# Three edits to a decode step with a streamed key and value cache: 8 KB runs per partition, a column-tiled projection, and the last key group loaded sooner

## The chip, the cores and the metric

One core of a Trainium2 chip. PE is its matrix engine (TensorE; PEld are its weight loads), DVE the vector engine, ACT the scalar engine, SPq the queue of the sync engine that issues the loads; PSUM holds the tiles that PE writes (ktp, S_ps, A_ps and others). The metric is device time in microseconds (us) of one execution. Beside the time, each profiled run has a *span*: from the first to the last instruction of the program. The time is about 1.8 us longer than the span (206.27 against 204.5 in the profiled run of the kernel before). Times are compared with times here, and spans with spans. The profiled run of the kernel before was a long one (206.27 us, where the median is 205.2), so gains of span against it are up to 1.1 us too large; the ratios are of times and do not have this fault.

## The reference, cut to what matters

```
def reference(A_x, A_k_cache, A_v_cache, A_wq, A_wo, B_x, B_w1, B_b1, B_w2, B_b2, gate_w):
    # 8 sequences, 1 query, 16 query heads on 8 key heads of 256, window = last 1024 of 4096 positions
    q = (x @ wq) per head
    k, v = last 1024 positions of the caches, each key head shared by 2 query heads
    a = softmax(q @ k.T / 16) @ v, heads joined, @ wo
    b = gelu(layernorm(x) @ w1 + b1) @ w2 + b2
    g = sigmoid((x * gate_w).sum(-1))
    return g * a + (1 - g) * b          # 8 x 448, bf16
```

wq and wo are the projections into and out of the attention, w1 and w2 the weights of the MLP b. What it costs to read: 64 MiB of keys and values and some 10 MB of weights, 77.7 MB in all, each byte used once.

## The kernel before

Everything is loaded through a ring of 8 KB-per-partition slots (1 MiB each), in one planned order, from one queue. Work on the caches goes in 16 *groups* of four key heads of one sequence; a group has two slots of keys and two of values.

```python
    def kv_loader(src, b, g):                    # one slot: two heads, 4 KB of each in a partition
        def load(t):
            nc.sync.dma_start(
                t[:].rearrange("p (a n) -> p a n", a=2),
                src[b, g : g + 2, kv_base:Sk, :].rearrange("a (p c) d -> p a (c d)", c=NC),
            )
    ...                                          # cut
    for u in range(1, NQ):                       # order of the loads (NQ = 16 groups)
        add_kv("k", A_k_cache, u)
        add_kv("v", A_v_cache, u - 1)
    add_kv("v", A_v_cache, NQ - 1)
    for q in range(NHQ):                         # then wo: three pieces of 896 KB, 448, 224, 224 KB
        ...
    for u in range(1, NQ):                       # the loop
        transpose_keys(u)                        # 64 PE transposes into PSUM, 8 copies out (5 DVE, 3 ACT)
        values(u - 1, *weights(u - 1))           # 64 value matmuls; 8 + 1 selection matmuls before them
        scores(u)                                # 16 matmuls of 512 columns, 4 column tiles of the PE
        softmax(u)                               # DVE maximum, ACT Exp of 1024 columns
    values(NQ - 1, *weights(NQ - 1))
    ...                                          # oT -> pp -> oP: heads regrouped for the projection by wo
    A_ps = ps_misc.tile([NB, D], F32, tag="misc", name="A_ps")
    for q in range(NHQ):
        for j0, j1 in WO_PARTS[q]:
            w = slot("wo", q, j0)
            for j in range(j0, j1):
                nc.tensor.matmul(A_ps[:, :], lhsT=oP[:, j, q, :],          # 8 rows, 448 columns
                                 rhs=w[:, (j - j0) * D : (j - j0 + 1) * D], ...)
    ...                                          # res = g * A_ps + mixb, stored by one DMA
```

## Time and profile before

The median of three runs was 204.73 us (204.66 to 205.67). Span of the profiled run: 204.5 us.

| what, kernel before | value | where it is read |
|---|---|---|
| DMA engines busy | 9 tenths from about 5 to 189 us, 408 GB/s | page, slices; windows |
| a 4096 B packet / an 8192 B packet (wq) | 164 / 311 ns, median | packet records of the trace |
| a group (4 MiB) | 10.2 us | spacing of key transposes |
| last piece of wo landed | 196.7 us | completion marks of the loads |
| projection A_ps | 192.66 to 201.39 us | timeline |

The span in 40 slices of 5.1 us, from the page of the kernel before: busy tenths of PE, granted PE clock, busy share of the DMA engines, and the rate.

```profile
PE   1898697879797979769797979797978797974793
PEclk9996589696969696966969696969696969695569
DMA  5999999999999999999999999999999999999710
GB/s 202 400 424 413 421 407 412 405 405 409 405 412 405 409 409 406 412 405 408 409 406 408 408 410 406 408 409 406 405 409 405 410 405 410 407 414 413 311 40 1
```

The DMA row is at 9 nearly to the end while PE breathes between 6 and 9, and the clock alternates between full and half: from 41 to 184 us the clock records have 1.0 for 6.8 us and 0.5 for 3.4 us by turns, with one longer half of 6.8 us at 88.6 us. In the windows view of the same kernel the last columns are the granted clock, the busy share of the 16 DMA engines (at 1.03 the durations of the packets sum to more than the time of 16 engines, so some overlap) and the rate.

```profile
core 0: us, PE busy (x) PEld busy (x) DVE busy (x) ACT busy (x) POOL busy (x), PEclk, DMA share, GB/s
50.00:75.00 25.00, 21.94 (x369) 17.82 (x368) 14.11 (x29) 11.08 (x14) 0.00 (x0) 0.84 1.03 408
100.00:150.00 50.00, 43.41 (x745) 38.11 (x743) 27.26 (x60) 21.20 (x25) 0.00 (x0) 0.83 1.03 408
```

So the load stream never pauses.

Last, the timeline of the tail (start, duration, engine, line):

```profile
192.18 0.42 DVE L468 CAST oP<-pp 128x256 bf16<-128x256 f32 x1 [0.59 <-PE pp L460]
192.66 8.72 PE L475 MATMUL A_ps<-slot,oP 128*8 128x448 bf16 x32 [0.57 <-DVE oP L468]
201.42 0.67 DVE L482 SCALAR_TENSOR_TENSOR res<-A_ps,g_sb,mixb 8x448 bf16<-8x448 f32 x1 [8.81 <-PE A_ps L475]
202.12 0.31 SPq L490 DMA_DIRECT2D out_dram<-res  x1
```

oP is ready at 192.6, the projection takes 8.7 us, and result and store follow. There are two candidates for what sets the time: the load stream, and the serial tail of compute after it.

### The profile page before, as it was taken

What the parts mean: (1) busy time and instruction counts of PE and PEld (TensorE: products, weight loads), DVE (VectorE), ACT (ScalarE), POOL (GpSimd) and SP (SyncE); (2) the same over time, 40 slices, a digit from 0 to 9 for tenths busy, and PEclk for the clock granted to TensorE, in tenths of its full rate; (3) what the DMA queues carried; (4) which work ended last, traced back from release to release, by engine and by line L of the source; (5) the groups of instructions that cost most, each with busy time, mean ns of one, the idle gap of its engine ahead of it and who ended that gap; (6) DMA issues with size and microseconds to landing.
All of it is one profiled execution on the core that took longest, in us unless ns stands there. A gap on an engine that the chain in (4) does not pass through costs nothing.

```text
span 204.5 us, 6049 instructions
## 1 busy us (share of the span) xinstructions
PE 166.6 (81%) x2734; PEld 133.1 (65%) x2734; DVE 94.3 (46%) x223; ACT 69.8 (34%) x85; POOL 0.8 (0%) x7
## 2 busy tenths in 40 slices
PE   1898697879797979769797979797978797974793
PEld 1798456566666666649595959595958667672531
DVE  6623046273737373706464646464645363633101
ACT  4330025070707070705261616161615343432000
POOL 1000000000000000000000000000000000000000
PEclk9996589696969696966969696969696969695569
DMA  5999999999999999999999999999999999999710
GB/s 202 400 424 413 421 407 412 405 405 409 405 412 405 409 409 406 412 405 408 409 406 408 408 410 406 408 409 406 405 409 405 410 405 410 407 414 413 311 40 1
DMA packets 19801, 78.07 MB, mean 382 GB/s; under 512 B 1440, under 2 KB 1856, under 8 KB 19392
## 3 DMA queue, kind: packets, MB, share of 16 engines
q1 hardware_dynamic: 19600, 77.68, 94.9%
q8 instruction: 21, 0.34, 0.7%
q10 hardware_dynamic: 176, 0.02, 0.1%
q14 instruction: 4, 0.03, 0.0%
HBM read 77.69 MB, written 0.01 MB: 380 GB/s over the span
## 4 chain that ended last, share of the span: by engine, by line
DMA 64%; PE 19%; DVE 8%; ACT 4%; issue 2%; SPq 2%; ACTq 0%
DMA slot<-in_A_k_cache_dram 29%; DMA slot<-in_A_v_cache_dram 28%; DMA slot<-in_A_wq_dram 7%; PE po L357 6%; PE S_ps L305 5%; PE A_ps L475 4%; DVE nmx L317 4%; DVE kt L270 3%; ACT E L320 2%; PE ktp L264 2%; ACT kt L268 2%; PE sm L340 1%; SPq L115 1%; SPq L96 1%; DVE selr L330 1%
## 5 line engine op out<-in xcount | busy, mean ns | idle before, releaser
L264 PEld LDWEIGHTS <-slot 128*128 128x128 bf16 x1024 | 76.0, 115 | 23.6 <-DMA slot<-in_A_k_cache_dram 16.0
L264 PE MATMUL ktp<-ident,slot 128*128 128x128 bf16 x1024 | 82.3, 250 | 9.6 <-DMA slot<-in_A_k_cache_dram 5.0
L270 DVE COPY kt<-ktp 128x1024 bf16<-128x1024 bf16 x80 | 53.1, 687 | 22.1 <-PE ktp L264 21.1
L268 ACT COPY kt<-ktp 128x1024 bf16<-128x1024 bf16 x48 | 47.8, 1012 | 25.0 <-PE ktp L264 24.9
L320 ACT ACTIVATE E<-S_ps,nmx 128x1024 bf16<-128x1024 f32 x16 | 17.8, 1113 | 84.3 <-DVE nmx L317 84.3
L357 PEld LDWEIGHTS <-slot 128*128 128x128 bf16 x1024 | 30.3, 99 | 9.7 <-issue 6.2
L357 PE MATMUL po<-ET,slot 128*128 128x2 bf16 x1024 | 29.3, 163 | 8.0 <-DVE ET L342 5.0
L317 DVE TENSOR_REDUCE nmx<-S_ps 128x1 f32<-128x1024 f32 x16 | 19.6, 1225 | 19.3 <-PE S_ps L305 19.3
L305 PE MATMUL S_ps<-kt,qw 128*2 128x512 bf16 x256 | 24.3, 516 | 0.4 <-DVE qw L291 0.4
L366 DVE TENSOR_TENSOR oT<-po,rb 128x8 bf16<-128x8 f32 x32 | 4.3, 189 | 32.5 <-PE po L357 32.5
L340 PE MATMUL sm<-selr,ones_f 128*128 128x8 f32 x32 | 6.4, 272 | 6.7 <-DVE selr L330 6.6
L340 PEld LDWEIGHTS sm<-selr,ones_f 128*128 128x128 f32 x32 | 5.0, 195 | 8.2 <-DVE selr L330 7.7
L305 PEld LDWEIGHTS <-qw 128*2 128x2 bf16 x256 | 5.4, 93 | 7.2 <-issue 4.5
L475 PE MATMUL A_ps<-slot,oP 128*8 128x448 bf16 x32 | 8.7, 449 | 0.6 <-DVE oP L468 0.6
L333 PE MATMUL sm<-sel,E 128*128 128x8 bf16 x128 | 5.5, 167 | 2.6 <-ACT E L320 2.6
L342 DVE CAST ET<-sm 128x64 bf16<-128x64 f32 x16 | 3.6, 224 | 8.0 <-PE sm L340 8.0
L333 PEld LDWEIGHTS <-E 128*128 128x128 bf16 x128 | 4.9, 97 | 3.5 <-ACT E L320 3.5
L475 PEld LDWEIGHTS <-oP 128*8 128x8 bf16 x32 | 3.3, 105 | 5.7 <-issue 3.4
L281 PE MATMUL qt<-xT,slot 128*128 128x8 bf16 x128 | 4.0, 168 | 2.3 <-DMA slot<-in_A_wq_dram 1.9
L281 PEld LDWEIGHTS <-slot 128*128 128x128 bf16 x128 | 3.8, 104 | 2.5 <-DMA slot<-in_A_wq_dram 2.2
L482 DVE SCALAR_TENSOR_TENSOR res<-A_ps,g_sb,mixb 8x448 bf16<-8x448 f32 x1 | 0.7, 670 | 8.8 <-PE A_ps L475 8.8
L330 DVE TENSOR_SCALAR selr<-sel,rsum 128x8 f32<-128x8 bf16 x16 | 3.7, 232 | 0.6
(58 smaller groups left out, 39.1 us busy)
## 6 DMA issues: line engine op xcount, KB each, us to landing
slot<-in_A_k_cache_dram SPq DMA_DIRECT2D x32, 1024.0 KB, 18.4
slot<-in_A_v_cache_dram SPq DMA_DIRECT2D x32, 1024.0 KB, 18.4
slot<-in_A_wq_dram SPq DMA_DIRECT2D x3, 1024.0 KB
slot<-in_A_wo_dram SPq DMA_DIRECT2D x3, 896.0 KB, 17.9
slot<-in_B_w_dram SPq DMA_DIRECT2D x1, 1008.0 KB, 16.3
slot<-in_B_w_dram SPq DMA_DIRECT2D x1, 896.0 KB, 9.0
slot<-in_B_w_dram SPq DMA_DIRECT2D x1, 560.0 KB, 15.5
slot<-in_A_wq_dram SPq DMA_DIRECT2D x1, 512.0 KB, 16.5
```

What stands on the lines that cost most here:

```text
L264: nc.tensor.transpose(ktp[:, c * P : (c + 1) * P], kn[:, o : o + P], ident[:])
L268: nc.scalar.copy(kt[:, j, :], ktp[:])
L270: nc.vector.tensor_copy(kt[:, j, :], ktp[:])
L281: nc.tensor.matmul(qt[:, k, :], lhsT=w[:, c : c + P], rhs=xT[:, r + half, :], start=(r == 0 and k == 0), stop=(r == NR), skip_group_check= ...
L305: nc.tensor.matmul(S_ps[32 * a : 32 * a + rep, hf * NMM : (hf + 1) * NMM], lhsT=qw[:, j, b, h0 : h0 + rep], rhs=KT[a][:, j, hf * NMM : (hf ...
L317: nc.vector.reduce_max(nmx[:], S_ps[:], axis=AXIS.X, negate=True)
L320: nc.scalar.activation(E[:], S_ps[:], ACT.Exp, bias=nmx[:], scale=1.0, accum_out=rowsum[:])
L330: nc.vector.tensor_scalar_mul(selr[:], sel[:], rsum[:])
L333: nc.tensor.matmul(sm[:, c, :], lhsT=E[:, c * P : (c + 1) * P], rhs=sel[:], start=True, stop=True,)
L340: nc.tensor.matmul(sm[:, NC, :], lhsT=ones_f[:], rhs=selr[:], start=True, stop=True)
L357: nc.tensor.matmul(PO[:, j, rep * a : rep * (a + 1)], lhsT=vn[:, o + j : o + Dh : NJ], rhs=ET[:, c, rep * a : rep * (a + 1)], start=(c == ...
L475: nc.tensor.matmul(A_ps[:, :], lhsT=oP[:, j, q, :], rhs=w[:, (j - j0) * D : (j - j0 + 1) * D], start=(q == 0 and j == 0), stop=(q == NHQ - ...
```

## The change: intent and diff

Three edits, marked R, T and O here. **R**: the two heads of a slot are interleaved over the partitions (even partitions one head, odd partitions the other), so that a partition reads one run of 8 KB instead of two of 4 KB. For that, Exp writes each column twice, a mask (`own`) drops the wrong head, and selection matmuls go from 8 to 16. **T**: the projections (and the MLP's second matmul) are cut into four column tiles of 112 columns, which run side by side; gate and bias follow them onto four partition blocks, and the store becomes four. **O**: the keys of group 15 are loaded and used one group sooner, before the last values.

```diff
R    def load(t):
         nc.sync.dma_start(
-            t[:].rearrange("p (a n) -> p a n", a=2),
-            src[b, g : g + 2, kv_base:Sk, :].rearrange("a (p c) d -> p a (c d)", c=NC),
+            t[:],
+            src[b, g : g + GP, kv_base:Sk, :].rearrange("a (s c) d -> s a (c d)", c=NCK),
         )
R   scores:
-                        rhs=KT[a][:, j, hf * NMM : (hf + 1) * NMM],
+                        rhs=KT[a // GP][:, j, hf * CMM : (hf + 1) * CMM, :, a % GP],
R   softmax:
-            E[:], S_ps[:], ACT.Exp, bias=nmx[:], scale=1.0, accum_out=rowsum[:]
+            E[:].rearrange("p (k a) -> p k a", a=GP),
+            S_ps[:].rearrange("p (k o) -> p k o", o=1).to_broadcast([P, W, GP]),
+            ACT.Exp, bias=nmx[:], scale=1.0, accum_out=rowsum[:],
R   weights:
-        for c in range(NC):
+        for c in range(NCK):                       # 16 selection matmuls instead of 8
-        nc.vector.tensor_copy(ET[:], sm[:, 0:NC, :])
+        nc.vector.tensor_tensor(ET[:], sm[:, 0:NCK, :], own..., op=ALU.mult)
O   loads:
-    for u in range(1, NQ):
-        add_kv("k", A_k_cache, u)
-        add_kv("v", A_v_cache, u - 1)
-    add_kv("v", A_v_cache, NQ - 1)
+    for u in range(1, NQ - 1):
+        add_kv("k", A_k_cache, u)
+        if u < NQ - 2:
+            add_kv("v", A_v_cache, u - 1)
+    add_kv("k", A_k_cache, NQ - 1)
+    for u in range(NQ - 3, NQ):
+        add_kv("v", A_v_cache, u)
O   the loop runs to NQ - 3, then (u = NQ - 2):
+    transpose_keys(u); W0 = weights(u - 1); scores(u); softmax(u)
+    transpose_keys(u + 1); W1 = weights(u); values(u - 1, *W0)
+    scores(u + 1); softmax(u + 1); values(u, *W1); values(u + 1, *weights(u + 1))
T   projection:
-                nc.tensor.matmul(A_ps[:, :], lhsT=oP[:, j, q, :],
-                                 rhs=w[:, (j - j0) * D : (j - j0 + 1) * D], ...)
+                for dst, cols in quads(A_ps):      # 4 x 112 columns, PSUM partitions 0, 32, 64, 96
+                    nc.tensor.matmul(dst, lhsT=oP[:, j, q, :],
+                                     rhs=w[:, o + cols.start : o + cols.stop], ...)
 ... (gate, bias, mlp_out, stores on the four blocks; ring of 18 slots instead of 19: cut)
```

More of the change, by code (lines that the diff above doesn't have):

```diff
@@ L56 @@
     NQ = NB * Hkv // QUAD
-    CD = NC * Dh
+    GP = 2
+    NCK = NC * GP
+    SK = P // GP
     SLOT = 4096
@@ L62 @@
     WO_PARTS = [[(0, NJ8)]] * (NHQ - 1) + [[(0, 4), (4, 6), (6, 8)]]
-    RING = 19
+    RING = 18
+    NMM = 512
+    CMM = NMM // SK
     qscale = float(Dh) ** -0.5
@@ L71 @@
     ring = ctx.enter_context(tc.tile_pool(name="ring", bufs=RING))
-    ktpool = ctx.enter_context(tc.tile_pool(name="ktpool", bufs=8))
-    epool = ctx.enter_context(tc.tile_pool(name="epool", bufs=2))
+    ktpool = ctx.enter_context(tc.tile_pool(name="ktpool", bufs=4))
+    epool = ctx.enter_context(tc.tile_pool(name="epool", bufs=3))
     ps_s = ctx.enter_context(tc.tile_pool(name="ps_s", bufs=1, space=PSUM))
@@ L96, in load @@
             nc.sync.dma_start(
-                t[:].rearrange("p (a n) -> p a n", a=2),
-                src[b, g : g + 2, kv_base:Sk, :].rearrange(
-                    "a (p c) d -> p a (c d)", c=NC
+                t[:],
+                src[b, g : g + GP, kv_base:Sk, :].rearrange(
+                    "a (s c) d -> s a (c d)", c=NCK
                 ),
@@ L161 @@
     gw_b = consts.tile([NB, D], BF16)
-    b2_b = consts.tile([NB, D], BF16)
+    b2_r = consts.tile([1, D], BF16)
     b1_sb = consts.tile([P, NF], BF16)
@@ L166 @@
     )
-    nc.scalar.dma_start(
-        b2_b[:], B_b2.rearrange("(o d) -> o d", o=1).to_broadcast([NB, D])
-    )
+    nc.scalar.dma_start(b2_r[:], B_b2.rearrange("(o d) -> o d", o=1))
     nc.scalar.dma_start(b1_sb[:], B_b1.rearrange("(p c) -> p c", c=NF))
@@ L180, with quads @@
     NX = NR + 2
+    DQ = D // QUAD
+    def quads(ps):
+        return [
+            (ps[32 * i : 32 * i + NB, :], slice(i * DQ, (i + 1) * DQ))
+            for i in range(QUAD)
+        ]
     xz = consts.tile([NB, 2, P], BF16)
@@ L189 @@
     oT = consts.tile([P, Hq, NJ, NB], BF16)
-    g_sb = consts.tile([NB, 1], F32)
-    omg = consts.tile([NB, 1], F32)
-    b2o = consts.tile([NB, D], F32)
-    mixb = consts.tile([NB, D], F32)
-    res = consts.tile([NB, D], BF16)
+    gg = consts.tile([NB, 2], F32)
+    spread = consts.tile([NB, QUAD, 32], F32)
+    gg_s = consts.tile([P, 2], F32)
+    ones_r = consts.tile([1, NB], BF16)
+    mixb = consts.tile([P, DQ], F32)
+    res = consts.tile([P, DQ], BF16)
+    nc.vector.memset(spread[:], 0.0)
+    nc.vector.memset(ones_r[:], 1.0)
     def transposed(dst, src, srcz):
@@ L209 @@
         ident[:].rearrange("p (a s) -> p a s", a=QUAD)[:, :, 0:rep],
+    )
+    par = consts.tile([P, GP], F32)
+    own = consts.tile([P, RQ], F32)
+    nc.vector.reduce_sum(
+        par[:], ident[:].rearrange("p (s a) -> p a s", a=GP), axis=AXIS.X
+    )
+    nc.vector.tensor_copy(
+        own[:].rearrange("p (t a i) -> p t a i", a=GP, i=rep),
+        par[:]
+        .rearrange("p (t a i) -> p t a i", t=1, i=1)
+        .to_broadcast([P, QUAD // GP, GP, rep]),
     )
@@ L246, in norm_and_gate @@
         nc.scalar.activation(gth[:], gl[:], ACT.Tanh, scale=0.5)
-        nc.vector.tensor_scalar(g_sb[:], gth[:], 0.5, 0.5, op0=ALU.mult, op1=ALU.add)
-        nc.vector.tensor_scalar(omg[:], g_sb[:], -1.0, 1.0, op0=ALU.mult, op1=ALU.add)
-        nc.vector.tensor_scalar_mul(b2o[:], b2_b[:], omg[:])
+        nc.vector.tensor_scalar(
+            gg[:, 0:1], gth[:], 0.5, 0.5, op0=ALU.mult, op1=ALU.add
+        )
+        nc.vector.tensor_scalar(
+            gg[:, 1:2], gth[:], -0.5, 0.5, op0=ALU.mult, op1=ALU.add
+        )
+        nc.vector.tensor_copy(
+            spread[:, :, 0:NB],
+            ident[0:NB, 0:NB]
+            .rearrange("p (o b) -> p o b", o=1)
+            .to_broadcast([NB, QUAD, NB]),
+        )
+        gp = ps_misc.tile([P, 2], F32, tag="misc", name="gp")
+        nc.tensor.matmul(
+            gp[:],
+            lhsT=spread[:].rearrange("p i b -> p (i b)"),
+            rhs=gg[:],
+            start=True,
+            stop=True,
+        )
+        nc.vector.tensor_copy(gg_s[:], gp[:])
     KT = {}
@@ L256, in transpose_keys @@
             kn = slot("k", u, s)
-            for a in range(2):
-                kt = ktpool.tile([P, NJ, W], BF16, tag="kt", name="kt")
-                KT[2 * s + a] = kt
+            kt = ktpool.tile([P, NJ, NCK, SK, GP], BF16, tag="kt", name="kt")
+            KT[s] = kt
+            ktf = kt[:].rearrange("p j c s a -> p j (c s a)")
+            for c0 in range(0, NCK, NC):
                 for j in range(NJ):
@@ L262, in transpose_keys @@
                     for c in range(NC):
-                        o = a * CD + c * Dh + j * P
+                        o = (c0 + c) * Dh + j * P
                         nc.tensor.transpose(
@@ L266, in transpose_keys @@
                         )
+                    dst = ktf[:, j, c0 * P : (c0 + NC) * P]
                     if evac[0] % 8 in (2, 4, 7):
-                        nc.scalar.copy(kt[:, j, :], ktp[:])
+                        nc.scalar.copy(dst, ktp[:])
                     else:
-                        nc.vector.tensor_copy(kt[:, j, :], ktp[:])
+                        nc.vector.tensor_copy(dst, ktp[:])
                     evac[0] += 1
@@ L295, in query @@
             )
-    NMM = 512
     def scores(u):
@@ L317, in softmax @@
         nc.vector.reduce_max(nmx[:], S_ps[:], axis=AXIS.X, negate=True)
-        E = epool.tile([P, W], BF16, tag="E", name="E")
+        E = epool.tile([P, W * GP], BF16, tag="E", name="E")
         rowsum = epool.tile([P, 1], F32, tag="rowsum", name="rowsum")
         nc.scalar.activation(
-            E[:], S_ps[:], ACT.Exp, bias=nmx[:], scale=1.0, accum_out=rowsum[:]
+            E[:].rearrange("p (k a) -> p k a", a=GP),
+            S_ps[:].rearrange("p (k o) -> p k o", o=1).to_broadcast([P, W, GP]),
+            ACT.Exp,
+            bias=nmx[:],
+            scale=1.0,
+            accum_out=rowsum[:],
         )
@@ L329, in weights @@
         selr = epool.tile([P, RQ], F32, tag="selr", name="selr")
-        nc.vector.tensor_scalar_mul(selr[:], sel[:], rsum[:])
-        sm = ps_sm.tile([P, NC + 1, RQ], F32, tag="sm", name="sm")
-        for c in range(NC):
+        nc.vector.tensor_scalar(
+            selr[:], sel[:], rsum[:], float(GP), op0=ALU.mult, op1=ALU.mult
+        )
+        sm = ps_sm.tile([P, NCK + 1, RQ], F32, tag="sm", name="sm")
+        for c in range(NCK):
             nc.tensor.matmul(
@@ L339, in weights @@
             )
-        nc.tensor.matmul(sm[:, NC, :], lhsT=ones_f[:], rhs=selr[:], start=True, stop=True)
-        ET = epool.tile([P, NC, RQ], BF16, tag="ET", name="ET")
-        nc.vector.tensor_copy(ET[:], sm[:, 0:NC, :])
+        nc.tensor.matmul(sm[:, NCK, :], lhsT=ones_f[:], rhs=selr[:], start=True, stop=True)
+        ET = epool.tile([P, NCK, RQ], BF16, tag="ET", name="ET")
+        nc.vector.tensor_tensor(
+            ET[:],
+            sm[:, 0:NCK, :],
+            own[:].rearrange("p (o r) -> p o r", o=1).to_broadcast([P, NCK, RQ]),
+            op=ALU.mult,
+        )
         rb = epool.tile([P, RQ], F32, tag="rb", name="rb")
-        nc.vector.tensor_copy(rb[:], sm[:, NC, :])
+        nc.vector.tensor_copy(rb[:], sm[:, NCK, :])
         return ET, rb
@@ L351, in values @@
             vn = slot("v", u, s)
-            for a2 in range(2):
-                a = 2 * s + a2
-                for j in range(NJ):
-                    for c in range(NC):
-                        o = a2 * CD + c * Dh
-                        nc.tensor.matmul(
-                            PO[:, j, rep * a : rep * (a + 1)],
-                            lhsT=vn[:, o + j : o + Dh : NJ],
-                            rhs=ET[:, c, rep * a : rep * (a + 1)],
-                            start=(c == 0),
-                            stop=(c == NC - 1),
-                        )
+            cols = slice(GP * rep * s, GP * rep * (s + 1))
+            for j in range(NJ):
+                for c in range(NCK):
+                    o = c * Dh + j
+                    nc.tensor.matmul(
+                        PO[:, j, cols],
+                        lhsT=vn[:, o : (c + 1) * Dh : NJ],
+                        rhs=ET[:, c, cols],
+                        start=(c == 0),
+                        stop=(c == NCK - 1),
+                    )
             done()
@@ L421, in mlp_out @@
     def mlp_out(hs):
-        bb = ps_misc.tile([NB, D], F32, tag="misc", name="bb")
+        bb = ps_misc.tile([P, DQ], F32, tag="misc", name="bb")
+        nc.vector.memset(bb[:], 0.0)
         for c in range(NF):
             w, o = (slot("w2", 0), c) if c < W2A else (slot("w2", 1), c - W2A)
-            nc.tensor.matmul(
-                bb[:, :],
-                lhsT=hs[:, c, :],
-                rhs=w[:, o * D : (o + 1) * D],
-                start=(c == 0),
-                stop=(c == NF - 1),
+            for dst, cols in quads(bb):
+                nc.tensor.matmul(
+                    dst,
+                    lhsT=hs[:, c, :],
+                    rhs=w[:, o * D + cols.start : o * D + cols.stop],
+                    start=(c == 0),
+                    stop=False,
+                )
+        for dst, cols in quads(bb):
+            nc.tensor.matmul(
+                dst, lhsT=ones_r[:], rhs=b2_r[:, cols], start=False, stop=True
             )
         done(2)
-        nc.vector.scalar_tensor_tensor(
-            mixb[:],
-            in0=bb[:],
-            scalar=omg[:],
-            in1=b2o[:],
-            op0=ALU.mult,
-            op1=ALU.add,
-        )
+        nc.vector.tensor_scalar_mul(mixb[:], bb[:], gg_s[:, 1:2])
     norm_and_gate()
@@ L448 @@
     mlp_out(hs)
-    for u in range(1, NQ):
+    for u in range(1, NQ - 2):
         transpose_keys(u)
@@ L453 @@
         softmax(u)
-    values(NQ - 1, *weights(NQ - 1))
+    u = NQ - 2
+    transpose_keys(u)
+    W0 = weights(u - 1)
+    scores(u)
+    softmax(u)
+    transpose_keys(u + 1)
+    W1 = weights(u)
+    values(u - 1, *W0)
+    scores(u + 1)
+    softmax(u + 1)
+    values(u, *W1)
+    A_ps = ps_misc.tile([P, DQ], F32, tag="misc", name="A_ps")
+    nc.vector.memset(A_ps[:], 0.0)
+    values(u + 1, *weights(u + 1))
     pp = ps_sm.tile([P, HPQ, NJ, NHQ, NB], F32, tag="sm", name="pp")
@@ L468 @@
     nc.vector.tensor_copy(oP[:], pp[:].rearrange("p m j q b -> p (m j) q b"))
-    A_ps = ps_misc.tile([NB, D], F32, tag="misc", name="A_ps")
     for q in range(NHQ):
@@ L474 @@
             for j in range(j0, j1):
-                nc.tensor.matmul(
-                    A_ps[:, :],
-                    lhsT=oP[:, j, q, :],
-                    rhs=w[:, (j - j0) * D : (j - j0 + 1) * D],
-                    start=(q == 0 and j == 0),
-                    stop=(q == NHQ - 1 and j == NJ8 - 1),
-                )
+                for dst, cols in quads(A_ps):
+                    o = (j - j0) * D
+                    nc.tensor.matmul(
+                        dst,
+                        lhsT=oP[:, j, q, :],
+                        rhs=w[:, o + cols.start : o + cols.stop],
+                        start=(q == 0 and j == 0),
+                        stop=(q == NHQ - 1 and j == NJ8 - 1),
+                    )
     nc.vector.scalar_tensor_tensor(
@@ L484 @@
         in0=A_ps[:],
-        scalar=g_sb[:],
+        scalar=gg_s[:, 0:1],
         in1=mixb[:],
@@ L489 @@
     )
-    nc.sync.dma_start(out_f, res[:])
+    for i, (src, cols) in enumerate(quads(res)):
+        eng = nc.sync if i % 2 == 0 else nc.scalar
+        eng.dma_start(out_f[:, cols], src)
 _INS = ['A_x', 'A_k_cache', 'A_v_cache', 'A_wq', 'A_wo', 'B_x', 'B_w1', 'B_b1', 'B_w2', 'B_b2', 'gate_w']
```

## The prediction

> **What bounds it now.** The busy tenths by slices show the 16 DMA engines at 9 from 5 to 188 us at 405-412 GB/s, for 78 MB. The windows view gives 408 GB/s in the steady part, 421 at 20-25 us, where wq arrives in 8 KB rows. In the packet records a 4096 B packet takes 164 ns (median), an 8192 B one 311 ns. One group (4 MiB of keys and values) takes 10.2 us of DMA.
>
> The compute loop is almost as long. In the timeline, groups start their key transposes 10.18-10.23 us apart at 40-84 us with no wait for a DMA: the chain of waits runs scores (1.8 us, at half clock) - maximum 1.24 - Exp 1.1+0.19 - ScalarE copy 0.9 - transposes 0.6 - two VectorE copies 1.3 - selection matmuls, ET - values 1.85. At 102-153 us, with the half clock falling on the transposes, the same loop waits 0.57 us for keys, so it needs about 9.65 us. From the first key transposes of group 14 (165.05 us) to the end are 39.4 us: the last two groups, then a serial tail: A_ps 8.73 us (32 matmuls of 448 columns, mostly at half clock), result 0.67, store 2.4.
>
> **What the change does.**
> 1. 8 KB runs: 64 MiB of keys and values at about 2.46-2.49 us a MiB instead of 2.55: 4-6 us less DMA, a group 9.85-9.95 us.
> 2. Price of it in compute: Exp writes each element twice. [...] Eight more selection pairs, about 42 ns each: +0.34 on PE; ET as a masked product +0.06. Value matmuls: still 64, with 4 columns. [...]
> The Exp lies on the loop: with the scores cold I estimate 11.1 us, with them warm 10.3, with the transposes cold (Exp half hidden) 10.0. Mean about 10.3, against 10.44 before (29.29 to 165.05 us, 13 groups). So the loop becomes compute-bound, DMA waits for ring slots, and most of the DMA gain is lost.
> 3. Projection in four column tiles: four matmuls of 112 columns side by side. Scores already run that way. 128 pairs at about 29 ns (the value pairs' rate) are 3.7 us: -5 us, all on the tail. Result on 128x112: -0.35. Four stores on two queues: +0.3.
> 4. Last keys sooner: group 15's transposes overlap group 14's softmax, values of 14 overlap softmax 15: by adding durations, -1 to -1.5 us.
>
> **Sum.** Group 14 starts at 29.3 + 13 x 10.3 = 163.2; the new tail takes 33.3 us: 196.5 us. If DMA alone bounded it, about 192. I say 196.0, range 191.5 to 201.5. Faster 0.83, same 0.14, slower 0.03.
>
> **What would show it.** 8 KB packets at 311 ns; DMA share under 0.97 in the steady part with PE not waiting for keys; [...] A_ps 3.5-4.5 us; group starts 10.2-10.5 us apart.
>
> **What would make it wrong.** The loop hides Exp better (then DMA-bound, 191-193); the half-clock stretches settle on the scores (11.1 us a group, 205); key packets alternating between two heads slower than wq's; strided kt reads slowing scores; column tiles serialising.

The sum came to 196.5 us, said as 196.0; the stride-two reads of kt the sum took as free. The loop's 11.1, 10.3 and 10.0 us a group, and so the 196.5 and the 205, contain the term for Exp. The trace after gives 0.855 us for it (1968 against 1113 ns) and 0.04 to 0.06 us for the reads. With this 0.855, the 0.06 of ET and the 10.2 us of the loop before, 11.1 is met again, and less the 0.84 us by which the scores of the kernel before are shorter at full clock (1.87 and 1.03 us), 10.3.

## More of the kernel before

In the groups of the page, the columns after the bar are busy time and mean ns of one, then the idle time of the engine before them and what ended most of it.

```profile
L264 PEld LDWEIGHTS <-slot 128*128 128x128 bf16 x1024 | 76.0, 115 | 23.6 <-DMA slot<-in_A_k_cache_dram 16.0
...
L320 ACT ACTIVATE E<-S_ps,nmx 128x1024 bf16<-128x1024 f32 x16 | 17.8, 1113 | 84.3 <-DVE nmx L317 84.3
...
L475 PE MATMUL A_ps<-slot,oP 128*8 128x448 bf16 x32 | 8.7, 449 | 0.6 <-DVE oP L468 0.6
```

PE's weight loads for the transposes wait mostly for keys (16.0 of the 23.6 us in which they sit idle). The projection at the end waits for oP, not for wo.

The runs of the kernel before lie between 204.3 and 206.4 us.

## The result, and the profile after

The changed kernel takes 198.79 us (median of 4, 198.76 to 199.07), the kernel before 205.2 us (median of 4). Ratio 0.969, interval 0.966 to 0.973: faster. A ratio here is the mean time of one kernel's fast runs over the mean of the other's fast runs of the same rounds, so it is not quite the ratio of the medians. The predicted time was 196.0, range 191.5 to 201.5.

The same slices (now of 4.9 us) for the kernel after:

```profile
PE   1699869868686878979596868686868686887662
PEclk9996556999999996799999999999999999997555
DMA  4999999999999999999999999999999999999960
GB/s 170 416 427 406 420 412 414 421 414 424 411 414 419 419 419 416 414 419 419 423 411 411 423 416 423 409 418 423 416 416 413 418 419 419 421 411 416 413 246 23
```

and the windows:

```profile
core 0: us, PE busy (x) PEld busy (x) DVE busy (x) ACT busy (x) POOL busy (x), PEclk, DMA share, GB/s
50.00:75.00 25.00, 18.38 (x367) 15.49 (x364) 13.34 (x28) 13.62 (x14) 0.00 (x0) 0.98 1.01 417
100.00:150.00 50.00, 37.62 (x782) 31.29 (x779) 26.68 (x60) 24.44 (x25) 0.00 (x0) 1.00 1.01 417
```

The clock is at full speed from 85 to 180 us (half from 16 to 33 us and after 180), PE is less busy, and the DMA engines are as saturated as before (share 1.01), at 417 instead of 408 GB/s. The clock is not what gained: the four runs of the kernel after had mean clocks of 0.81, 0.85, 0.87 and 0.90 and times within 0.31 us of each other.

The groups that answer to those above:

```profile
L311 PEld LDWEIGHTS <-slot 128*128 128x128 bf16 x1024 | 66.1, 105 | 33.3 <-issue 28.3
...
L366 ACT ACTIVATE E<-S_ps,nmx 128x2048 bf16<-128x2048 f32 x16 | 31.5, 1968 | 72.2 <-DVE nmx L363 72.2
...
L545 PE MATMUL A_ps<-slot,oP 128*8 128x112 bf16 x128 | 4.3, 290 | 2.8 <-DMA slot<-in_A_wo_dram 2.1
```

Exp takes 1968 ns where it took 1113. Of the 33.3 us in which the weight loads of the transposes sit idle, 28.3 are "issue", waiting that the profile cannot name, so at most 5.0 are a wait for keys (16.0 before); and A_ps now waits for wo. The tail in the timeline:

```profile
186.90 0.42 DVE L537 CAST oP<-pp 128x256 bf16<-128x256 f32 x1 [0.59 <-PE pp L529]
187.38 1.15 PE L545 MATMUL A_ps<-slot,oP 128*8 128x112 bf16 x32 [0.57 <-DVE oP L537]
188.97 0.92 PE L545 MATMUL A_ps<-slot,oP 128*8 128x112 bf16 x32 [0.44 <-DMA slot<-in_A_wo_dram]
191.17 0.92 PE L545 MATMUL A_ps<-slot,oP 128*8 128x112 bf16 x32 [1.28 <-DMA slot<-in_A_wo_dram]
192.31 1.01 PE L545 MATMUL A_ps<-slot,oP 128*8 128x112 bf16 x24 [0.22 <-DMA slot<-in_A_wo_dram]
193.48 0.36 PE L545 MATMUL A_ps<-slot,oP 128*8 128x112 bf16 x8 [0.16 <-DMA slot<-in_A_wo_dram]
193.89 0.34 DVE L552 SCALAR_TENSOR_TENSOR res<-A_ps,gg_s,mixb 128x112 bf16<-128x112 f32 x1 [6.57 <-PE A_ps L545]
194.25 0.68 SPq L562 DMA_DIRECT2D out_dram<-res  x2
```

oP is ready 5.3 us sooner, and A_ps then sits waiting for each piece of wo: it runs when the pieces land, and ends 0.4 us after the last of them (193.44). The end of the chain of waits says the same (start, duration, what):

```profile
159.60 19.96 DMA slot<-in_A_v_cache_dram
179.62 13.82 DMA slot<-in_A_wo_dram
193.48 0.39 PE A_ps L545 x6
193.89 0.34 DVE res L552
```

Finally, what the DMA engines moved. Packets, and those that the page lists as `instruction`, before:

```profile
DMA packets 19801, 78.07 MB, mean 382 GB/s; under 512 B 1440, under 2 KB 1856, under 8 KB 19392
...
q8 instruction: 21, 0.34, 0.7%
```

and after:

```profile
DMA packets 11645, 78.10 MB, mean 396 GB/s; under 512 B 1489, under 2 KB 1890, under 8 KB 3042
...
q8 instruction: 23, 0.38, 0.8%
```

Packets fell from 19801 to 11645. In the packet records, an 8192 B packet took 313 ns (median) in the kernel after, against 164 ns for one of 4096 B before: 4.6% less per byte by these durations, but packets overlap (the share fell from 1.03 to 1.01), and the rate rose by 2.2%. The `instruction` lines matter later.

A table that the views do not print, worked out from the completion marks of each load (each has sixteen; a load is taken as landed at the last of them, and the transposes of the kernel before start 0.05 to 0.23 us after it in the table) and from the starts of the key transposes. "Lag" is the time from the landing of a group's first keys to the first transpose of them:

| group | 3 | 5 | 6 | 7 | 9 | 12 | 13 | 14 | 15 |
|---|---|---|---|---|---|---|---|---|---|
| before: keys landed, us | 49.64 | 70.06 | 80.26 | 92.03 | 112.42 | 143.05 | 153.23 | 165.00 | 175.23 |
| before: lag | 0.20 | 0.20 | 0.21 | 0.23 | 0.05 | 0.05 | 0.05 | 0.05 | 0.05 |
| after: keys landed, us | 49.22 | 69.16 | 79.20 | 90.65 | 110.69 | 140.60 | 152.05 | 162.04 | 167.02 |
| after: lag | 0.23 | 0.62 | 1.58 | 0.31 | 0.61 | 1.22 | 0.05 | 0.11 | 3.17 |

Before, compute starts on every group within 0.25 us of the landing: it follows the stream. After, the stream delivers a group every 9.98 us and the loop takes 10.17, so the lag grows by 0.2 us a group (by 1.0 in group 5, which met a stretch of half clock at 74 us), and is reset twice, where the landings themselves jump by 1.5 us (79.20 to 90.65 is 11.45 us for one group; before it is 80.26 to 92.03 and 153.23 to 165.00). The 3.17 us at group 15 are edit O, which has these keys landed half a group sooner. Two questions follow. Why does a loop that is slower than the stream not cost time? And what are the jumps?

### The profile page after: what moved, and what is told of

Its sections match the earlier page's. It is cut to its first block, busy times and chain, and to the rows that moved or that the text cites. A ratio compares the mean times of both kernels' runs of the same rounds, so it can differ in the third digit from the quotient of the medians.

```text
span 197.0 us, 6578 instructions
## 1 busy us (share of the span) xinstructions
PE 147.7 (75%) x3006; PEld 125.1 (64%) x3006; DVE 94.3 (48%) x230; ACT 82.0 (42%) x85; POOL 0.9 (0%) x7
## 4 chain that ended last, share of the span: by engine, by line
DMA 49%; PE 26%; DVE 16%; ACT 5%; issue 2%; SPq 0%; ACTq 0%
DMA slot<-in_A_v_cache_dram 31%; PE ktp L311 10%; DMA slot<-in_A_wq_dram 8%; DVE kt L318 7%; PE po L414 7%; DMA slot<-in_A_wo_dram 7%; DVE nmx L363 6%; PE S_ps L351 5%; ACT kt L316 4%; DMA slot<-in_A_k_cache_dram 3%; PE sm L393 2%; ACT E L366 1%; DVE ET L395 1%; DVE selr L381 1%; PE bb L484 1%
## 5 line engine op out<-in xcount | busy, mean ns | idle before, releaser
L311 PE MATMUL ktp<-ident,slot 128*128 128x128 bf16 x1024 | 73.9, 232 | 21.6 <-ACT kt L316 15.2
L311 PEld LDWEIGHTS <-slot 128*128 128x128 bf16 x1024 | 66.1, 105 | 33.3 <-issue 28.3
L366 ACT ACTIVATE E<-S_ps,nmx 128x2048 bf16<-128x2048 f32 x16 | 31.5, 1968 | 72.2 <-DVE nmx L363 72.2
L414 PEld LDWEIGHTS <-slot 128*128 128x128 bf16 x1024 | 29.5, 99 | 6.8 <-issue 6.8
L414 PE MATMUL po<-ET,slot 128*128 128x4 bf16 x1024 | 28.1, 164 | 5.3 <-DVE ET L395 5.3
L351 PE MATMUL S_ps<-kt,qw 128*2 128x512 bf16 x256 | 18.1, 402 | 0.4 <-DVE qw L339 0.4
L386 PE MATMUL sm<-sel,E 128*128 128x8 bf16 x256 | 8.8, 167 | 1.7 <-ACT E L366 1.7
L386 PEld LDWEIGHTS <-E 128*128 128x128 bf16 x256 | 8.2, 97 | 1.8 <-ACT E L366 1.8
L395 DVE TENSOR_TENSOR ET<-sm,own 128x128 bf16<-128x128 f32 x16 | 4.7, 291 | 8.2 <-PE sm L393 8.2
L351 PEld LDWEIGHTS <-qw 128*2 128x2 bf16 x256 | 4.7, 82 | 5.2 <-DVE qw L339 0.5
L545 PE MATMUL A_ps<-slot,oP 128*8 128x112 bf16 x128 | 4.3, 290 | 2.8 <-DMA slot<-in_A_wo_dram 2.1
L329 PEld LDWEIGHTS <-slot 128*128 128x128 bf16 x128 | 3.7, 104 | 1.0 <-DMA slot<-in_A_wq_dram 0.6
```

What stands on the lines that cost most here:

```text
L311: nc.tensor.transpose(ktp[:, c * P : (c + 1) * P], kn[:, o : o + P], ident[:])
L329: nc.tensor.matmul(qt[:, k, :], lhsT=w[:, c : c + P], rhs=xT[:, r + half, :], start=(r == 0 and k == 0), stop=(r == NR), skip_group_check= ...
L351: nc.tensor.matmul(S_ps[32 * a : 32 * a + rep, hf * NMM : (hf + 1) * NMM], lhsT=qw[:, j, b, h0 : h0 + rep], rhs=KT[a // GP][:, j, hf * CMM ...
L366: nc.scalar.activation(E[:].rearrange("p (k a) -> p k a", a=GP), S_ps[:].rearrange("p (k o) -> p k o", o=1).to_broadcast([P, W, GP]), ACT.Exp,
L386: nc.tensor.matmul(sm[:, c, :], lhsT=E[:, c * P : (c + 1) * P], rhs=sel[:], start=True, stop=True,)
L395: nc.vector.tensor_tensor(ET[:], sm[:, 0:NCK, :], own[:].rearrange("p (o r) -> p o r", o=1).to_broadcast([P, NCK, RQ]), op=ALU.mult,)
```

## The experiments

Two theories were set against each other. **D**: the load stream sets the time up to the landing of the last piece of wo; after it comes a tail. **C**, my prediction's: the compute loop and its serial tail set it, and the doubled Exp takes most of the DMA gain back. Later came **F**: the jumps in the landings come with the 16384 B packets that the page lists as `instruction` on q8 (21 before, 23 after; the recorded texts call them pages), of which the first, the 9th and the 17th stand out; so the jumps are gone without PE instructions, and come later and fewer with less of them. The kernels with one or two of the three edits were built from the two kernels by taking over all hunks of the marked edits and leaving the others. Ratios are to the kernel before in the same call, with their 95% interval; with a line drawn at 2%, e1 to e4 and e6 count as "same" and e10 as "unclear", so those differences are read from the intervals and the traces.

### One edit or two of the three

**e1_tiles_only**: the kernel before with edit T.

```diff
-                nc.tensor.matmul(A_ps[:, :], ...)               # 448 columns
+                for dst, cols in quads(A_ps): nc.tensor.matmul(dst, ...)   # 4 x 112
```

> The kernel before with the column-tiled projection alone (4 KB runs, old order). Theory D (the DMA stream sets the time up to the landing of the last piece of wo, then a short tail): last piece of wo lands where it did before, 196.7 us, A_ps waits for it, about 3.6 us of tail: span 200 to 200.8, ratio to before 0.980. Rival C (the compute loop and its serial tail set the time): oP still ready at 192.6, A_ps 4.3 us without a wait for wo, span 200.4. The times agree; the theories differ in the wait: D sees A_ps end its idle time on wo landings, C does not.

Measured: span 200.3, time 202.28 us, ratio 0.985 [0.980, 0.990]. A_ps starts at 193.05, the last piece of wo lands at 196.90, A_ps ends at 197.21:

```profile
193.05 2.56 PE L503 MATMUL A_ps<-slot,oP 128*8 128x112 bf16 x96 [0.57 <-DVE oP L495]
195.81 0.95 PE L503 MATMUL A_ps<-slot,oP 128*8 128x112 bf16 x24 [0.20 <-DMA slot<-in_A_wo_dram]
196.94 0.27 PE L503 MATMUL A_ps<-slot,oP 128*8 128x112 bf16 x8 [0.18 <-DMA slot<-in_A_wo_dram]
```

The last two bursts wait for wo. That is D.

**e2_runs_only**: the kernel before with edit R.

```diff
-                src[...].rearrange("a (p c) d -> p a (c d)", c=NC)
+                src[...].rearrange("a (s c) d -> s a (c d)", c=NCK)
```

> The kernel before with 8 KB runs alone (old order, old projection). Both theories: last piece of wo lands at about 193.4 us, 3.3 earlier, but the old serial tail hides most of it: group starts 10.17 us apart put group 15 at about 172.3, its scores end at 182.5, oP at 190.5, A_ps of 8.7 to 10 us follows: span 202 to 203.5, ratio 0.990 to 0.995. If the DMA gain counted in full here: span 201.2 or less.

Measured: span 203.3, time 204.97 us (202.31 to 205.29), ratio 0.995 [0.987, 1.003]: the same within the noise. The last landing came at 192.50, 4.2 us sooner than before (0.9 sooner than expected; a group took 9.93 us), and the old projection hides it:

```profile
191.16 9.01 PE L502 MATMUL A_ps<-slot,oP 128*8 128x448 bf16 x32 [0.57 <-DVE oP L495]
```

**e3_order_only**: the kernel before with edit O.

```diff
-    for u in range(1, NQ):       transpose, values(u - 1), scores, softmax
+    for u in range(1, NQ - 2):   the same; the last two groups interleaved
```

> The kernel before with the last key group sooner alone (4 KB runs, old projection). Last value slot lands at about 188, oP at about 190.3 instead of 192.6; A_ps of 32 matmuls at 0.27 to 0.37 us, most at half clock, 8.7 to 11.9 us: span 202 to 205, ratio 0.988 to 1.002. Theory D: small, as the projection still runs after the last landing. Rival C: my prediction's 1 to 1.5 us, span 203.

Measured: span 201.3, a little under the range expected, time 203.52 us, ratio 0.992 [0.986, 0.998]. A_ps starts at 190.40 instead of 192.66, which is 2.3 us; it also runs 0.9 us shorter, and that is the clock and not the order (see the table below). The last landing stays at 196.75.

**e6_no_runs**: the kernel after without edit R (so T and O).

```diff
-                t[:], src[...].rearrange("a (s c) d -> s a (c d)", c=NCK)
+                t[:].rearrange("p (a n) -> p a n", a=2), src[...].rearrange("a (p c) d -> p a (c d)", c=NC)
```

> The kernel after with the 4 KB runs of before (column tiles and new order kept, Exp not doubled). Theory D: last landing back at 196.7 us, tail 3.6 as after: span 200.3, 3.3 us over after, ratio to before 0.980. Rival C (my prediction: the doubled Exp takes back most of the DMA gain): a shorter Exp pays for the longer DMA, span within 1 us of after's 197.0.

Measured: span 200.8, time 202.37 us, ratio 0.985 [0.981, 0.990]. From its page:

```profile
L349 ACT ACTIVATE E<-S_ps,nmx 128x1024 bf16<-128x1024 f32 x16 | 17.8, 1114 | 79.5 <-DVE nmx L346 79.5
...
L517 PE MATMUL A_ps<-slot,oP 128*8 128x112 bf16 x128 | 4.0, 291 | 3.4 <-DMA slot<-in_A_wo_dram 3.2
```

Exp is back at 1.11 us, and nothing is gained by it: A_ps waits for wo, the last landing is at 197.31 and A_ps ends at 197.71. Against the kernel after the span is 3.8 us longer; C had expected the two within 1 us. C falls here.

**e4_no_tiles**: the kernel after without edit T (so R and O).

```diff
-                for dst, cols in quads(A_ps): nc.tensor.matmul(dst, ...)
+                nc.tensor.matmul(A_ps[:, :], ...)
```

> The kernel after with the old projection of 32 matmuls of 448 columns (8 KB runs and new order kept). oP ready at 187.4 us as after, then 8.7 us (clock as before) to 11.9 us (all at half clock), result 0.67, store 2.4: span 199.2 to 202.4, 2 to 5.4 us over after's 197.0. If the tiles were worth nothing because wo lands late (last at 193.4): span 197 to 198.

Measured: span 200.2, time 202.92 us (201.92 to 204.31), ratio 0.987 [0.980, 0.995]. The last landing is at 192.60, A_ps runs from 189.66 to 197.05.

**e5_no_order**: the kernel after without edit O (so R and T).

```diff
-    the last two groups interleaved
+    for u in range(1, NQ): transpose, values(u - 1), scores, softmax
```

> The kernel after with the old order of the last groups (8 KB runs and column tiles kept). Group 15 starts at about 172.3, oP is ready at 190.5 to 191.1, A_ps 4.3 us with hardly a wait for wo: A_ps ends at about 195.4 instead of 193.9, span 198.4, 1.4 us over after. Rival: if everything waits for the last landing at 193.4 whatever the order, span 197.0 to 197.3.

Measured: span 197.1, time 199.31 us (198.76 to 200.47), ratio 0.971 [0.965, 0.978]. The rival expectation was right: the order is worth nothing beside the other two. oP came at 190.70 as expected, but the projection needs only 3.2 us once all its weights are there, and ends at 193.9 with the last landing (193.61):

```profile
190.70 3.22 PE L531 MATMUL A_ps<-slot,oP 128*8 128x112 bf16 x128 [0.57 <-DVE oP L523]
```

All eight combinations in one table (us, from the traces; "need" is how long A_ps ran where it did not wait for wo at the end):

| edits | A_ps starts | last wo lands | A_ps ends | span | ratio of times |
|---|---|---|---|---|---|
| none (before) | 192.66 | 196.74 | 201.39 (need 8.7) | 204.5 | 1 |
| R | 191.16 | 192.50 | 200.17 (need 9.0) | 203.3 | 0.995 |
| O | 190.40 | 196.75 | 198.23 (need 7.8) | 201.3 | 0.992 |
| R O | 189.66 | 192.60 | 197.05 (need 7.4) | 200.2 | 0.987 |
| T | 193.05 | 196.90 | 197.21 | 200.3 | 0.985 |
| T O | 190.90 | 197.31 | 197.71 | 200.8 | 0.985 |
| R T | 190.70 | 193.61 | 193.92 (need 3.2) | 197.1 | 0.971 |
| R T O (after) | 187.38 | 193.44 | 193.84 | 197.0 | 0.969 |

One sum fits every row: A_ps ends at the later of (its start plus its need) and (the last landing plus 0.3 to 0.4), and the span ends 3.1 us after that. With the old projection the first term is the later one, and R is worth 1.1 to 1.2 us of span; with the tiled one the second is, and R is worth 3.2 us beside T alone, 3.8 beside T and O. O helps only while the first term rules.

The need of the old projection differs between rows (8.72, 9.01, 7.82, 7.39 us), and the clock records of these four traces say why. Of it 5.11, 5.69, 3.29 and 2.41 us fell on the half clock (before, R, O, R O); a matmul of 448 columns started every 373 ns there and every 190 ns at full clock. Counting half-clock time half, the need is 6.16, 6.16, 6.18 and 6.18 us: the same in every row. The tiled one needs 3.2 us although most or all of it fell on the half clock (2.8 of 3.2 us in R T, all 3.2 in e10 below).

One column was not foreseen. T itself moves the last landing later: by 0.2 and 0.6 us without R (before to T, O to T O), by 1.1 and 0.8 us with it (R to R T, R O to R T O). With R, a group comes every 9.98 us instead of 9.93 to 9.94. The traces of e7, e8 and e10 agree with the kernel after within 0.1 us here. Why T does this was not tested.

### Is the loop on the path?

**e7_exp_once**: less ScalarE work in the loop. Wrong: the odd columns' weights are not those that belong there.

```diff
-            E[:].rearrange("p (k a) -> p k a", a=GP), S_ps[:]...to_broadcast([P, W, GP]), ACT.Exp,
+            E[:], S_ps[:], ACT.Exp,
-                lhsT=E[:, c * P : (c + 1) * P],
+                lhsT=E[:, (c % NC) * P : (c % NC + 1) * P],
```

> The kernel after with Exp writing 1024 columns once and the selection matmuls reading them twice: WRONG RESULT ON PURPOSE, same matmuls, ScalarE 0.85 us a group less. Theory D: the loop needs about 9.4 us a group without waits and now waits for keys, group starts follow the DMA, 9.98 us apart; last landing and span stay at 193.4 and 197.0 within 0.4 us. Rival C (my prediction: the doubled Exp costs time on the loop): span falls towards 192.

Measured: span 197.0, time 198.91 us, ratio 0.968 [0.963, 0.972]. Group starts are 9.8 to 10.5 us apart except at the two jumps, the lag is never over 0.6 us until the last group; last landing 193.50. From its page:

```profile
L366 ACT ACTIVATE E<-S_ps,nmx 128x1024 bf16<-128x1024 f32 x16 | 17.8, 1113 | 79.7 <-DVE nmx L363 79.7
...
L545 PE MATMUL A_ps<-slot,oP 128*8 128x112 bf16 x128 | 4.0, 290 | 3.4 <-DMA slot<-in_A_wo_dram 2.8
```

D is confirmed: a loop that is faster by 0.85 us of Exp gains nothing. (The comparison with the reference passed this kernel as correct all the same, and e9 below too. So it is not sensitive to errors in the attention weights of this problem.)

**e8_exp_longer**: more of it.

```diff
+        junk = epool.tile([P, 512], BF16, tag="junk", name="junk")
+        nc.scalar.activation(junk[:], S_ps[:, 0:512], ACT.Exp, bias=nmx[:], scale=1.0)
         soft[u] = (E, rowsum)
```

> The kernel after with one more Exp of 512 columns into a scratch tile after each softmax, about 0.6 to 0.7 us more ScalarE time a group on the loop; result stays right. Theory D says that the loop of 10.17 us is only just hidden, with some 2 us of slack at the end (A_ps waits 2.1 us in all for wo): 13 groups x 0.6 = 8 us, less 2: span 202 to 204, group starts 10.75 us apart. If the loop had real slack: span stays at 197.

Measured: span 197.1, time 199.29 us (198.85 to 201.59), ratio 0.971 [0.964, 0.979]. The expectation was wrong. Group 14 starts at 164.51 instead of 162.15 and A_ps at 190.31 instead of 187.38, and all of it is absorbed: the last landing is at 193.53 and A_ps ends at 193.93. Two things had been mis-sized. The slack is larger: A_ps needs 3.2 us, so in the kernel after it could start at 190.6, 3.3 us later than it does. And the edit was not clean. In the kernel after the sixth tile of transposes waits for a ScalarE copy, behind Exp:

```profile
64.00 1.52 PE L311 MATMUL ktp<-ident,slot 128*128 128x128 bf16 x24 [1.19 <-ACT kt L316]
```

in e8 for a VectorE copy:

```profile
63.76 1.31 PE L311 MATMUL ktp<-ident,slot 128*128 128x128 bf16 x16 [0.34 <-DVE kt L318]
```

so part of the longer Exp came off the loop. It looks as if the framework had given the transposes other PSUM buffers; the views leave buffer numbers out, so this is not shown. Two of the four runs were slower, by 0.9 and 2.7 us, as they would be if the slack was about used up.

**e10_exp_longer2**: more still, into a tile outside the rotating pool.

```diff
+    junk = consts.tile([P, W], BF16)
+        nc.scalar.activation(junk[:], S_ps[:], ACT.Exp, bias=nmx[:], scale=1.0)
         soft[u] = (E, rowsum)
```

> The kernel after with a further Exp of 1024 columns into a scratch tile after each softmax, about 1.02 us more ScalarE time a group; result right. e8 with 0.6 us more started group 14 2.4 us later than after and still ended at 197.1, with A_ps starting at 190.3 where after had 187.4. The slack left there is about 0.5 us, so here the loop must show: group starts about 11 us apart, group 14 at about 172, span 204 to 208. If the span stays at 197, the loop is not near the critical path at all.

Measured: span 206.8, time 209.11 us, ratio 1.021 [1.015, 1.028] of two runs; result correct. Group starts are 10.0 to 11.6 us apart, the lag grows to 14.8 us at group 15, the loads still finish at 193.50, and A_ps starts at 200.44 with all its weights there:

```profile
200.44 3.16 PE L547 MATMUL A_ps<-slot,oP 128*8 128x112 bf16 x128 [0.57 <-DVE oP L539]
```

Now the loop rules. The clock is no rival here: the mean was 0.79, and a run of the kernel after at 0.81 took 198.76 us. That brackets it: about 3 us of lag at the end is free, and the loop of the kernel after uses 0.2 us of it a group. It also answers the first question: the stream was never held up by a slower loop, not even here.

### The loads alone, and the jumps

**d1_loads_4k** and **d2_loads_8k**: the loads of the kernel before and after, no compute. Wrong (the output is zero).

```diff
-    norm_and_gate() ... res = g * A_ps + mixb
+    for i in range(len(plan)):
+        nc.vector.tensor_copy(touched[:], slots[i][:, 0:1])
+        done()
```

> The loads of the kernel before by themselves: same plan, ring and queue, each slot touched by one VectorE copy of one column; WRONG RESULT ON PURPOSE. The stream of 4 KB packets is what it is without any compute: 2.55 us a MiB. If the compute loop had ever held the stream back in the kernel before, the last landing would come well before 196.7 us. Theory F [...]: without PE instructions the 1.5 us jumps are gone and the last landing is 192.2 to 194.0. Without F: 196.0 to 196.9.

> The same for the kernel after; WRONG RESULT ON PURPOSE. 8 KB packets, 2.495 us a MiB. Theory F: last landing 189.0 to 190.7 instead of 193.4. Without F: 193.0 to 193.5. In either case 3.2 to 3.6 us earlier than the 4 KB loads of the same call: that is the gain of the longer runs by itself.

Measured, two timed runs each: last landings at 193.80 (d1) and 189.10 (d2), spans 196.8 and 192.1, times 198.62 and 193.80 us. The rates in 40 slices, d1:

```profile
GB/s 193 398 416 419 410 410 411 409 409 410 410 411 408 411 409 411 406 410 410 410 409 411 409 411 407 410 411 410 408 411 411 410 408 411 411 410 408 422 405 31
```

and d2:

```profile
GB/s 166 407 423 423 406 421 425 421 421 423 421 423 418 425 420 425 420 420 420 423 418 421 423 423 423 420 425 421 421 420 421 421 423 421 423 423 421 418 406 38
```

The longer runs are worth 4.7 us by themselves, 2.56 against 2.49 us a MiB. In the full kernels 3.3 us of it are seen. Of the kernels, the one before ends its loads 2.9 us later than its loads alone need, the one after 4.3 us later. Both last landings lie in the range of theory F and out of that of theory "no F", but the difference between the two, 4.7 us, is above the 3.2 to 3.6 expected. In both of these runs one smaller jump, of 1.0 and 0.6 us at about 83 us, is left; neither has a PE instruction or a packet on q8, and what it is stays open.

The traces have the packets on q8 in order, 16384 B and about 1.07 us each (1.02 to 1.11); their durations repeat every eight packets, within 11 ns before and 20 ns after. The completion marks step with them. Every load has sixteen marks (the records do not say which engine set a mark or carried a packet, so how a packet delays a landing is not shown). In the loads alone the last mark comes 0.4 to 0.5 us after the first (1.4 and 1.1 after the small jump). In the kernel before this spread is 0.8 us ahead of the first packet and 2.0 after it; it then stays at 2.1 to the ninth, which makes it 3.6, and the 17th makes it 5.2. Between these two the number of marks that come 3 us or more late is one after the ninth packet and grows by one with each packet to eight after the 16th. In the kernel after the spread goes from 0.4 to 2.0, 3.3 and 4.9. The ten other traces with work on PE step with the same packets, that of e9 below only twice. So the first packet comes with a delay too: the first keys of group 1 land at 29.24 us in both kernels, at 27.88 and 27.95 in their loads alone. Why a packet of 1.07 us goes with a delay of up to 1.6 stays open.

The 9th and the 17th packet, and the interval between two groups' first keys (9.98 us undisturbed after, 10.2 before) in which they fall:

| kernel | PE and PEld instructions | 16 KB packets, instructions to one | 9th packet, jump | 17th packet, jump |
|---|---|---|---|---|
| before | 2 x 2734 = 5468 | 21, 260 | 86.6 us; 80.26 to 92.03 (+1.6) | 154.6; 153.23 to 165.00 (+1.6) |
| after | 2 x 3006 = 6012 | 23, 261 | 82.1 us; 79.20 to 90.65 (+1.5) | 144.4; 140.60 to 152.05 (+1.5) |
| e9 | 2 x 1918 = 3836 | 15, 256 | 113.1 us; 109.53 to 121.06 (+1.5) | none |

**e9_fewer_instr** is the test: fewer PE instructions, same loads. Its output is wrong, which doesn't matter for the time.

```diff
-                for c in range(NCK):        # values: 64 matmuls a group
+                for c in range(1):          # 4
-        for c in range(NCK):                # selection: 16
+        for c in range(NC):                 # 8
```

> The kernel after with 4 instead of 64 value matmuls and 8 instead of 16 selection matmuls a group, some 2170 PE instructions less (about 15 pages of instructions instead of 23); same loads; WRONG RESULT ON PURPOSE. Theory F: no page 17, so one jump of 1.5 us less: last landing 191.9 us, span 195.5. Rival: the jumps belong to the load stream or to time, not to the instructions: last landing 193.4, span 197.0, as the lighter ScalarE of e7 left it.

Measured: span 195.8, time 197.48 us, ratio 0.964 [0.961, 0.968] of two runs. The packets on q8, from the page of e9:

```profile
q8 instruction: 15, 0.25, 0.5%
```

The first jump moved by 31 us, together with the ninth packet (82.1 to 113.1 us), and the second is gone. Every other interval is 9.97 or 9.98 us. The last landing is at 192.29 instead of 193.44: 1.15 us sooner, where F had 1.5 and its rival 0. (From the first keys of group 1 on, the gain is 1.6 us; those landed 0.5 us later here, which stays open.) F holds, for when the jumps come and for how large they are. A second case came unplanned: e10 has the instructions of the kernel after, but in its slower loop the 17th packet came at 153.0 us instead of 144.4, and the second jump came one group later. The lighter loop is no rival cause, as e7 showed.

A version that beats the kernel after, with fewer PE instructions and a right result, was not built.

## Why the prediction was right or wrong, point by point

The time lay within the range (198.79, range 191.5 to 201.5), at 2.8 us over the value given. Part of that is bookkeeping: the time is about 1.8 us longer than the span of the same run, which the prediction left out. But the sum agreed for a partly wrong reason, and to that extent by luck.

1. **8 KB runs, "4-6 us less DMA, a group 9.85-9.95 us": right by themselves, too large beside T.** Alone R has 9.93 us a group and the last landing 4.2 us sooner (e2). In the kernel after it is 9.98 us a group, 2.495 us a MiB, last landing 3.3 us sooner (196.74 to 193.44), as T takes 0.8 to 1.1 us of it back, for a reason that was not tested. The 8192 B packet took 313 ns where I had put 311. Loads without any compute gain 4.7 us (d1, d2).
2. **Compute costs: right.** Exp 1968 ns, 855 more than before. ET 291 ns against 224 before (+0.07, predicted +0.06). The eight more selection pairs cost 0.20 us, not 0.34 (0.54 against 0.34 us for the row of them). Reading kt with a stride of two, which the sum took as free, is nearly so: 16 score matmuls at full clock 1.07 to 1.09 us against 1.03 before and in e6, 4 to 6% longer.
3. **"So the loop becomes compute-bound, DMA waits for ring slots, and most of the DMA gain is lost": the step that failed.** The first third is right (10.17 us against the stream's 9.98). But the DMA share was 1.01, not under 0.97: a lag of 0.2 us a group is no wait for a slot. It stays in the ring, the stream's own jumps reset it, and 3.3 us of it are free at the end. The DMA gain counted in full (e6: 3.8 us of span beside T and O). e7 and e10 show it from both sides.
4. **"If DMA alone bounded it, about 192": mis-sized, and this hid the failure of 3.** DMA alone did bound it, at a span of 197.0, a time of 198.8. The prediction put the gain of the loads at 4 to 6 us, and it was 3.3; after the last landing (193.44) still come 0.4 us of projection and 3.1 us of result and store, which the figure of 192 did not spell out.
5. **Column tiles, "-5 us, all on the tail": right, with a cap that I did not name.** The tiles run side by side: need 3.2 us instead of 7.4 to 9.0 (3.7 predicted). But below a need of about 4 us the last landing takes over: alone T is worth 4.2 us of span, 3.5 of median time (e1), beside R and O 3.2 of span (e4).
6. **Order, "-1 to -1.5 us": wrong beside the others.** Alone it starts A_ps 2.3 us sooner; span falls by 3.2 (e3), 0.9 of which is the clock. Beside R and T it gives 0.1 (e5), beside T alone nothing (e6 against e1). It makes oP ready 3.3 us sooner in the kernel after, and A_ps then waits for wo.
7. **Half clock as a risk: it did not matter to the kernel after.** I had spread the loop over three cases by where the half clock falls. The profiled run had full clock in most of the loop; other runs had not, with the same time. It did slow loops (in e4 four groups that met it took 10.7 to 11.0 us instead of 10.17), but the slack hid that; and it is what made the old projection need 7.4 to 9.0 us instead of 6.2.

Points 3 and 6 erred in opposite directions: the loop was charged too much, the order credited too much.

## What to carry to other kernels

Write the end of a streamed kernel as the later of two times, "last bytes landed plus what must still be done with them" and "compute ready plus what it still needs", and ask of every edit which of the two it moves; two edits that each gain little can gain much together (R 0.5%, T 1.5%, R and T 2.9%, each within about 0.8%), and a third can be worth nothing then. A compute loop slightly slower than the stream costs nothing until its summed lag exceeds the slack at the end (here 0.2 us a group against 3.3 us): sum the lag over the loop before you call the loop the bound. When landings jump, look at what else the DMA engines carry: here a fully unrolled program of 6012 PE and PEld instructions had 23 instruction packets of 16384 B, and with 3836 and 15 packets (e9) the last landing came 1.15 us sooner.
